# Attention scores from split keys: the second products on half the array's rows, copies of keys in place of copies of queries, and a new order

## The chip, the cores and the metric

The kernel runs on one core of one Trainium2 chip. The metric is device time in microseconds (us) of one execution. A core has TensorE (PE in the profile; PEld are its weight loads), VectorE (DVE), ScalarE (ACT), GpSimd (POOL), and SyncE (SP), whose queue issues nearly all of this kernel's transfers.

## The reference

The program is a sliding-window attention with sinks, followed by a two-layer network. All of it is float32.

```python
batch, n_heads, seq, head_dim = (4, 8, 768, 64)
n_sink, window = (4, 128)
scores = scale * np.matmul(q, k.transpose(0, 1, 3, 2))
keep = is_sink | in_window                  # first 4 keys, or the last 128 keys up to this one
scores = np.where(keep, scores, -1000000000.0)
a = softmax over keys;  x = a @ v           # heads side by side: 3072 tokens x 512
h = x @ w_in                                # 512 x 1024
solu = h * softmax(h);  ln = layer norm of solu, times g_ln
out = ln @ w_out                            # 1024 x 512
```

## The kernel before

**Tiles.** The work is cut into 24 windows `n` of 128 tokens: four batches of six. A window looks at its own 128 keys, the 128 keys before and the four sinks. So a score row of one head has 264 columns: two segments of `SEG` = 132 (four sink columns and 128 keys each). The first window of a batch has 128 columns alone.

**Split float32.** Each float32 factor is written as two numbers of the type fp32r, a first part (rounded to that type) and a second part (what is left), and a product is a sum of products of parts. A head has 64 dimensions, and the array has 128 rows, so two parts of a head fit above each other.

- `take_q` (ScalarE) writes the first part of four heads' queries into 64 rows of the tile `qT`, `rest_q` (VectorE) their second part into the other 64 rows. `x` (0 or 1) says which half holds the first part; `row_of` maps a head to `x` and its place `r`.
- `take_k` (ScalarE) and `rest_k` (GpSimd) do the same for keys in `ring`, a tile with four slots for windows' keys.
- `swap_q` copies `qT` with its halves exchanged into `qX`, by two DMAs of SP.
- `score` multiplies twice for each head, each time with 128 rows: `qT` by `ring` (first by first plus second by second), then `qX` by `ring` (second by first plus first by second). Both add into one bank of PSUM.

The first windows of batches 0 and 1 (`native`) are scored in plain float32 with 64 rows instead, by `qf` and `kf` (L654).

**After the scores.** There are two banks for scores, `bank_0` and `bank_1`; `claim` takes one and `done` gives it back. `pick` (L663) and `mask` (L674), both VectorE, merge the two segments, add the mask and find the row's maximum; then the bank is free. `exps` (ScalarE), `normalise` (GpSimd), a transposition of the probabilities (by DMA and VectorE, `store_p`, `load_p`, `flip_p`, or by TensorE), and `value` (L795), which multiplies by the values with 64 columns of the array for each of two heads. `hidden` (L815) and `project` (L902) are the network's two layers, three products of 512 columns for each block of weights.

**Order.** Every step is a function of `(n, i)`. A table of numbers, `ORDER`, lists all steps, and each engine runs its instructions in that order. So products of `hidden` and `project` of earlier windows stand between the scores of later ones.

Of the kernel before, what the change touches and what calls it, by code (L numbers as in the profile page):

```python
# [216 lines left out]
def _banded(ctx, tc, q, k, v, n_sink, window, w_in, w_out, g_ln, out, val, wts, wpool, consts):  # L217
# [264 lines left out]
    for b in range(B):  # L482
        upper = 1 if b == 1 else 0
        for c in range(NC):
# [6 lines left out]
            else:  # L491
                free = [x for x in (2 * up, 2 * up + 1) if (2, 0) not in slots or b > 1 or x != slots[2, 0]]
                slots[b, c] = free[c // 2 % len(free)]

    ring = cpool.tile([P, H, 4, SEG], F32R, name="ring")
    nc.vector.memset(ring.bitcast(F32)[:, :, 2:4, 0:NSK], 0.0)

    def slot_of(n):
# [622 lines left out]
```

## Time and profile before

| | |
|---|---|
| Time, median of 3 runs | 439.52 us (438.94 to 439.88) |
| The profiled execution | 439.91 us, of which the span is 437.9 us |
| TensorE busy | 415.4 us (95%) |
| VectorE busy | 360.9 us (82%) |
| ScalarE busy | 315.7 us (72%) |
| GpSimd busy | 234.2 us (53%) |
| DMA queue q1 | 80.77 MB, 82.3% of 16 engines' span |

The profile is of one execution. Busy times count an instruction from its start to its modelled end; products of TensorE overlap, so their rate is read from the distances of their starts. A row of the timeline gives the start in us from the span's start, the duration, the engine, the line and operation, `out<-in`, the part of the array (rows\*columns), shape, and how many instructions it merges; in brackets stands the idle time ahead of it and what ended it. A product of plain float32 leaves two records.

### The profile page before, as it was taken

To read this page: it belongs to the slowest core of one execution; us is meant where nothing else is said; L and a number is where in the kernel's file an instruction comes from. 1 tells how busy PE (TensorE), PEld (TensorE's weight loads), DVE (VectorE), ACT (ScalarE), POOL (GpSimd) and SP (SyncE) were. 2 spreads that over 40 slices of the span, in tenths; PEclk is the share of its full clock that TensorE was granted. 3 is DMA by queue.
4 is the path that set the end of the run, shared out by engine and by line. 5 is a ranking of instruction groups with operands and counts; after the bars stand their busy time and mean duration, and the time that the engine had idled before them with its cause. 6 is when DMAs were issued, how large, how long until landed. Compare 5 with 4: busy or idle time off the path is not lost.

```text
span 437.9 us, 8516 instructions
## 1 busy us (share of the span) xinstructions
PE 415.4 (95%) x2507; PEld 332.6 (76%) x2507; DVE 360.9 (82%) x1029; ACT 315.7 (72%) x817; POOL 234.2 (53%) x388
## 2 busy tenths in 40 slices
PE   4899999999999999999999999999999999999994
PEld 3447777878787888878777787878878778888884
DVE  2989999997999889999989997899899797674520
ACT  5989988978877776877768576768767675555551
POOL 7742626658867552788454736556623673624020
PEclk9999999999999999999999999999999999999999
DMA  8999449999899899976998989966966558623001
GB/s 225 324 284 293 96 101 168 180 151 196 218 161 216 208 185 253 195 229 190 180 239 210 207 219 226 193 173 179 269 176 216 170 165 227 188 96 121 24 26 55
DMA packets 164025, 81.38 MB, mean 186 GB/s; under 512 B 120188, under 2 KB 150788, under 8 KB 163972
## 3 DMA queue, kind: packets, MB, share of 16 engines
q1 hardware_dynamic: 163972, 80.77, 82.3%
q8 instruction: 22, 0.36, 0.4%
q14 instruction: 31, 0.25, 0.2%
HBM read 45.62 MB, written 23.72 MB: 158 GB/s over the span
## 4 chain that ended last, share of the span: by engine, by line
PE 53%; DVE 25%; DMA 6%; issue 5%; POOL 4%; ACT 4%; SPq 1%; DVEq 0%; POOLq 0%; ACTq 0%
PE o L902 18%; PE h L815 17%; PE av L795 5%; DVE qT L600 4%; DVE sc L674 3%; DVE bank L663 3%; PE bank L656 3%; PE bank L657 2%; PE ws L443 2%; DMA pb<-pd 2%; DVE ul L890 2%; DVE nm L820 2%; PE bank L654 2%; DMA wraw<-in_moe_w_in_dram 1%; DVE pt L725 1%
## 5 line engine op out<-in xcount | busy, mean ns | idle before, releaser
L685 ACT ACTIVATE sc<-sc,nmx 128x132 f32<-128x132 f32 (+1 forms) x192 | 75.9, 396 | 25.1 <-DVE nmx L674 24.1
L902 PE MATMUL o<-w2h,uh 128*128 128x512 f32 (+1 forms) x200 | 79.7, 398 | 0.0
L815 PE MATMUL h<-w1h,xh 128*128 128x512 f32 x192 | 77.0, 401 | 1.0 <-DVE u L830 0.9
L902 PE MATMUL o<-w2h,ul 128*128 128x512 f32 (+1 forms) x200 | 77.0, 385 | 0.5 <-DVE ul L890 0.5
L902 PE MATMUL o<-w2l,uh 128*128 128x512 f32 (+1 forms) x200 | 77.2, 386 | 0.0
L815 PE MATMUL h<-w1h,xl 128*128 128x512 f32 x192 | 75.9, 395 | 0.6 <-DVE xl L804 0.5
L815 PE MATMUL h<-w1l,xh 128*128 128x512 f32 x192 | 75.3, 392 | 0.0
L625 POOL TENSOR_TENSOR ring<-kf,ring 64x512 fp32r<-64x512 f32 x48 | 63.1, 1320 | 22.6 <-ACT ring L620 18.7
L674 DVE CUSTOM_DVE_ANT_0 sc<-bank,bias 128x132 f32<-128x132 f32 (+1 forms) x192 | 53.1, 288 | 9.4 <-PE bank L654 1.7
L704 POOL TENSOR_TENSOR pn<-sc,rs 128x512 f32<-128x512 f32 x26 | 28.0, 1079 | 53.1 <-DVE rs L691 19.2
L656 PE MATMUL bank<-ring,qT 128*128 128x264 f32 (+1 forms) x176 | 51.0, 300 | 1.9 <-DVE nmx L674 1.7
L657 PE MATMUL bank<-ring,qX 128*128 128x264 f32 (+1 forms) x176 | 48.3, 284 | 0.1
L700 POOL TENSOR_TENSOR sc<-sc,rs 128x528 f32<-128x528 f32 (+1 forms) x22 | 24.8, 1127 | 40.8 <-DVE rs L691 24.0
L902 PEld LDWEIGHTS o<-w2h,ul 128*128 128x128 f32 x200 | 37.5, 188 | 9.2 <-DVE ul L890 1.2
L902 PEld LDWEIGHTS o<-w2h,uh 128*128 128x128 f32 x200 | 37.6, 188 | 8.8 <-issue 3.1
L741 POOL TENSOR_SCALAR_AFFINE_SELECT pc<-pt 128x512 f32<-128x512 f32 x40 | 28.4, 716 | 29.4 <-DVE pt L725 25.5
L815 PEld LDWEIGHTS h<-w1h,xl 128*128 128x128 f32 x192 | 36.0, 188 | 10.6 <-DVE xl L804 2.8
L656 PEld LDWEIGHTS bank<-ring,qT 128*128 128x128 f32 x176 | 33.1, 188 | 12.0 <-DVE nmx L674 6.3
L815 PEld LDWEIGHTS h<-w1h,xh 128*128 128x128 f32 x192 | 36.1, 188 | 7.3 <-issue 0.8
L902 PEld LDWEIGHTS o<-w2l,uh 128*128 128x128 f32 x200 | 37.7, 188 | 5.0
L825 ACT ACTIVATE e<-h,nm 128x1024 f32<-128x1024 f32 x24 | 26.7, 1113 | 18.7 <-DVE nm L820 18.6
L815 PEld LDWEIGHTS h<-w1l,xh 128*128 128x128 f32 x192 | 36.2, 188 | 5.0
(146 smaller groups left out, 975.9 us busy)
## 6 DMA issues: line engine op xcount, KB each, us to landing
qX<-qT SPq DMA_DIRECT2D x88, 128.0 KB, 2.7
ud<-u SPq DMA_DIRECT2D x20, 512.0 KB, 4.3
ub<-ud SPq DMA_DIRECT2D x80, 128.0 KB, 3.5
pd<-pn SPq DMA_DIRECT2D x26, 256.0 KB, 3.0
pb<-pd SPq DMA_DIRECT2D x52, 128.0 KB, 3.4
vn<-in_v_dram SPq DMA_DIRECT2D x24, 256.0 KB, 4.3
out_dram<-ob SPq DMA_DIRECT2D x23, 256.0 KB, 2.6
kn<-in_k_dram SPq DMA_DIRECT2D x12, 384.0 KB, 6.6
```

The costliest lines, as they stand in the source:

```text
L625: nc.gpsimd.tensor_tensor(t[ROWS[1 - x]], src[ROWS[x]], t[ROWS[x]].bitcast(F32), op=ALU.subtract)
L656: nc.tensor.matmul(o, st["qT", n, x][:, r, :], rhs, start=True, stop=False)
L657: nc.tensor.matmul(o, st["qX", n, x][:, r, :], rhs, start=False, stop=True)
L674: nc.vector.tensor_tensor_reduce(out=st["sc", n, hb][:, j, c0:c1], in0=st["s", n, h].rearrange("p a x -> p (a x)")[:, c0:c1], in1=bias0 if ...
L685: nc.scalar.activation(sc[:, i, c0:c1], sc[:, i, c0:c1], AF.Exp, bias=nmx[:, i:i + 1], scale=-1.0, accum_out=ssum[:, i:i + 1])
L700: nc.gpsimd.tensor_tensor(sc[:, :, c0:c1], sc[:, :, c0:c1], rs.unsqueeze(2).to_broadcast([P, HB, c1 - c0]), op=ALU.mult)
L704: nc.gpsimd.tensor_tensor(pn.rearrange("p g h f -> p h g f"), sc[:, :, 4:SEG].rearrange("p h (g f) -> p h g f", f=32), rs.unsqueeze(2).uns ...
L741: nc.gpsimd.affine_select(pc, st["pt", n, hb], pattern=[[0, HB], [1, P]], compare_op=ALU.is_ge, fill=0.0, base=0, channel_multiplier=-1)
L795: nc.tensor.matmul(acc[ROWS[x], r, :], vals[:, 2 * r + x, :], p[:, 2 * jp + x, :], start=alone, stop=alone or (r, i) == (NPAIR - 1, 1))
L815: nc.tensor.matmul(st["h", n][:, cols], a[:, kt, :], w[:, kt, cols], start=(kt == 0 and m == 0), stop=(kt == KT1 - 1 and m == 2))
L825: nc.scalar.activation(e, st["h", n], AF.Exp, bias=st["nm", n], scale=1.0, accum_out=se)
L902: nc.tensor.matmul(st["o", n, i], a[:, kt % 4, :], part(w, kt)[:, i * wide:(i + 1) * wide], start=(kt == 0 and m == 0), stop=(kt == KT2 - ...
```

## The change

**Keys.** `ring` now holds the first part of a key in both halves: `take_k` writes one half, and the new `swap_k` copies it into the other by one DMA. The second part goes to a new tile, `ring_lo`, with each of two heads in its own half of the rows. `qX` and `swap_q` are gone.

**Scores.** `score` multiplies once with 128 rows: `qT` by `ring` (first by first plus second by first). The new step `cross` runs for a pair of heads, one in each half of the rows: two products of 64 rows, the first part of the queries by `ring_lo` (first by second). Second by second is left out of the sum.

**Heads.** For a pair, the two heads must stand in different halves; `row_of` now alternates in every window, `spot` finds a head's place afterwards, and `value` and `sinks_hi`/`sinks_lo` read their tiles by it. `skt` has one buffer instead of two. `ring_sinks` also copies the sink columns of `ring_lo`.

**Order.** `ORDER` is another table. On TensorE, before, in the middle of the kernel, a head's two products stand together, with products of `hidden` (`h`) around them:

```order
L815 MATMUL h_2219<-w1h,xl_2215 128x512
L656 MATMUL bank_89<-ring,qT_0_2017 128x264
L657 MATMUL bank_89<-ring,qX_0_2032 128x264
L815 MATMUL h_2219<-w1h,xh_2190 128x512
L815 MATMUL h_2219<-w1l,xh_2190 128x512
L815 MATMUL h_2219<-w1h,xl_2215 128x512
```

One bank is filled at a time. After, two heads' first products fill both banks, and the two products of 64 rows (L679, by `ring_lo`) follow:

```order
L674 MATMUL bank_89<-ring,qT_1_2019 128x264
L674 MATMUL bank_90<-ring,qT_0_2169 128x264
L679 MATMUL bank_90<-ring_lo,qT_0_2169 128x264
L679 MATMUL bank_89<-ring_lo,qT_1_2019 128x264
L842 MATMUL h_2261<-w1h,xh_2242 128x512
L842 MATMUL h_2261<-w1l,xh_2242 128x512
L842 MATMUL h_2261<-w1h,xl_2254 128x512
```

The second products of a pair moved together, behind both first ones. On SP, before, in the middle of the kernel, pairs of query copies stand between the other transfers:

```order
L867 DMA ub_2097<-ud_2022 32x4x256
L609 DMA qX_0_2228<-qT_0_2165 64x512
L610 DMA qX_0_2228<-qT_0_2165 64x512
L609 DMA qX_1_2237<-qT_1_2170 64x512
L610 DMA qX_1_2237<-qT_1_2170 64x512
L913 DMA out_dram<-ob_0_2172 128x512
```

After, single copies within `ring` stand there:

```order
L736 DMA pd_2151<-pn_0_2119 512x1x128
L631 DMA ring<-ring 64x4x128
L940 DMA out_dram<-ob_0_2159 128x512
L894 DMA ub_2198<-ud_2140 32x4x256 x2
```

Four copies for a window became two, on the keys' side.

The diff, without the rest of the table and the steps that only follow the heads' new places:

```diff
 ORDER = (
-    346, 0, 143, 2, 144, 244, 60, 348, 351, 5, 6, 3, 69, 350, 7, 51, 8, 352, 24, 9, 147, 154, 345, 12, 42, 155, 353,
...
+    ring_lo = cpool.tile([P, NPAIR, 4, SEG], F32R, name="ring_lo")
...
     def row_of(n, h):
-        return divmod(h, 2)[::-1] if turned(n) else divmod(h, NPAIR)
+        return divmod(h, 2)[::-1]
...
+    def spot(n, h):
+        return h if place(n)[0] == 0 else h % NPAIR * 2 + h // NPAIR
...
-    def swap_q(n, x):
-        if native(n):
-            return
-        t = st["qT", n, x]
-        o = st["qX", n, x] = sb.tile([P, NPAIR, P], F32R, tag="qX", name=f"qX_{n}_{x}", bufs=3)
-        nc.sync.dma_start(o.bitcast(F32)[0:D], t.bitcast(F32)[D:P])
-        nc.sync.dma_start(o.bitcast(F32)[D:P], t.bitcast(F32)[0:D])
...
+    def swap_k(n, x):
+        t = keys_of(n, x).bitcast(F32)
+        nc.sync.dma_start(t[ROWS[1 - x]], t[ROWS[x]])
+
     def rest_k(n, x):
-        t = keys_of(n, x)
         src = st["kf" if turned(n) else "kt", n]
-        nc.gpsimd.tensor_tensor(t[ROWS[1 - x]], src[ROWS[x]], t[ROWS[x]].bitcast(F32), op=ALU.subtract)
+        nc.gpsimd.tensor_tensor(ring_lo[ROWS[x], :, slot_of(n), 4:SEG], src[ROWS[x]],
+                                keys_of(n, x)[ROWS[x]].bitcast(F32), op=ALU.subtract)
...
+            nc.gpsimd.tensor_copy(ks[:, H:], ring_lo[:, :, first, 4:4 + NSK].bitcast(F32))
...
+                    nc.gpsimd.tensor_copy(ring_lo[:, :, slot, 0:NSK], st["ksink", b][:, H:].bitcast(F32))
...
+    def operands(n, h):
+        slot = slot_of(n)
+        x, r = row_of(n, h)
+        s = st["s", n, h]
+        if place(n)[1] == 0:
+            return s[:, 0, 4:SEG], ring[:, h, slot, 4:SEG], ring_lo[ROWS[x], r, slot, 4:SEG]
+        pslot = slot_of(before(n))
+        s0, s1 = min(slot, pslot), max(slot, pslot)
+        both = slice(s0, s1 + 1, s1 - s0)
+        return s, ring[:, h, both, :], ring_lo[ROWS[x], r, both, :]
+
     def score(n, h):
...
         nc.tensor.matmul(o, st["qT", n, x][:, r, :], rhs, start=True, stop=False)
-        nc.tensor.matmul(o, st["qX", n, x][:, r, :], rhs, start=False, stop=True)
+
+    def cross(n, r):
+        for x in range(2):
+            o, _, rhs = operands(n, 2 * r + x)
+            nc.tensor.matmul(o, st["qT", n, x][ROWS[x], r, :], rhs, start=False, stop=True)
...
-            skt = st["skt", n] = sb.tile([P, NPAIR, P], F32R, tag="skt", name=f"skt_{n}", bufs=2)
+            skt = st["skt", n] = sb.tile([P, NPAIR, P], F32R, tag="skt", name=f"skt_{n}", bufs=1)
```

More of the change, by code (lines that the diff above doesn't have):

```diff
@@ L495, in _banded @@
     ring = cpool.tile([P, H, 4, SEG], F32R, name="ring")
+    ring_lo = cpool.tile([P, NPAIR, 4, SEG], F32R, name="ring_lo")
     nc.vector.memset(ring.bitcast(F32)[:, :, 2:4, 0:NSK], 0.0)
+    nc.vector.memset(ring_lo.bitcast(F32)[:, :, 2:4, 0:NSK], 0.0)
     def slot_of(n):
@@ L507, in row_of @@
     def row_of(n, h):
-        return divmod(h, 2)[::-1] if turned(n) else divmod(h, NPAIR)
+        return divmod(h, 2)[::-1]
     def heads_of(n, x):
-        return slice(x, H, 2) if turned(n) else slice(NPAIR * x, NPAIR * (x + 1))
+        return slice(x, H, 2)
+    def spot(n, h):
+        return h if place(n)[0] == 0 else h % NPAIR * 2 + h // NPAIR
     def load(n, i, nm, src):
@@ L519, in load @@
         if turned(n):
-            nc.sync.dma_start(t.rearrange("p (c h d) -> p c h d", h=H, d=D)[:, region(n)],
-                              src[b, :, c * P:(c + 1) * P, :].rearrange("h p d -> p h d"))
+            to = t.rearrange("p (c h d) -> p c h d", h=H, d=D)[:, region(n)]
+            rows = src[b, :, c * P:(c + 1) * P, :].rearrange("h p d -> p h d")
+            if b == 0:
+                nc.sync.dma_start(to, rows)
+                return
+            for x in range(2):
+                nc.sync.dma_start(to[:, heads_of(n, x)], rows[:, NPAIR * x:NPAIR * (x + 1)])
             return
@@ L524, in load @@
         nc.sync.dma_start(t.rearrange("p (m d) -> p m d", d=32)[32 * i:32 * (i + 1)],
-                          src[b, heads_of(n, x), :, 32 * y:32 * (y + 1)].rearrange("h (t p) d -> p (h t) d", p=32))
+                          src[b, NPAIR * x:NPAIR * (x + 1), :, 32 * y:32 * (y + 1)].rearrange("h (t p) d -> p (h t) d", p=32))
     def load_k(n, i):
@@ L631, in ring_sinks @@
             first = slots[b, 0]
-            ks = st["ksink", b] = sb.tile([P, H, NSK], F32R, tag="ksink", name=f"ksink_{b}", bufs=2)
-            nc.gpsimd.tensor_copy(ks, ring[:, :, first, 4:4 + NSK].bitcast(F32))
+            ks = st["ksink", b] = sb.tile([P, H + NPAIR, NSK], F32R, tag="ksink", name=f"ksink_{b}", bufs=2)
+            nc.gpsimd.tensor_copy(ks[:, 0:H], ring[:, :, first, 4:4 + NSK].bitcast(F32))
+            nc.gpsimd.tensor_copy(ks[:, H:], ring_lo[:, :, first, 4:4 + NSK].bitcast(F32))
             fresh = [first] + fresh
@@ L637, in ring_sinks @@
                 if slot < 2:
-                    nc.gpsimd.tensor_copy(ring[:, :, slot, 0:NSK], st["ksink", b].bitcast(F32))
+                    nc.gpsimd.tensor_copy(ring[:, :, slot, 0:NSK], st["ksink", b][:, 0:H].bitcast(F32))
+                    nc.gpsimd.tensor_copy(ring_lo[:, :, slot, 0:NSK], st["ksink", b][:, H:].bitcast(F32))
     def cols_of(c):
         return (4, SEG) if c == 0 else (0, OFF)
-    def score(n, h):
-        slot = slot_of(n)
-        pslot = slot if place(n)[1] == 0 else slot_of(before(n))
-        s0, s1 = min(slot, pslot), max(slot, pslot)
-        s = st["s", n, h] = claim(("s", n, h), 1)[:, 0:2 * SEG].rearrange("p (a x) -> p a x", x=SEG)
-        if place(n)[1] == 0:
-            o, rhs = s[:, 0, 4:SEG], ring[:, h, slot, 4:SEG]
-        else:
-            o, rhs = s, ring[:, h, s0:s1 + 1:s1 - s0, :]
+    def operands(n, h):
[8 more added lines that the diff above has]
+        return s, ring[:, h, both, :], ring_lo[ROWS[x], r, both, :]
+    def score(n, h):
+        st["s", n, h] = claim(("s", n, h), 1)[:, 0:2 * SEG].rearrange("p (a x) -> p a x", x=SEG)
+        o, rhs, _ = operands(n, h)
         x, r = row_of(n, h)
@@ L656, in score @@
         nc.tensor.matmul(o, st["qT", n, x][:, r, :], rhs, start=True, stop=False)
-        nc.tensor.matmul(o, st["qX", n, x][:, r, :], rhs, start=False, stop=True)
+    def cross(n, r):
+        for x in range(2):
+            o, _, rhs = operands(n, 2 * r + x)
+            nc.tensor.matmul(o, st["qT", n, x][ROWS[x], r, :], rhs, start=False, stop=True)
     def pick(n, h):
@@ L748, in part_old, with sinks_of, sink_part @@
                                     fill=0.0, base=-1, channel_multiplier=1)
+    def sinks_of(n, hb, t):
+        sk = st["sk", n]
+        if place(n)[0] == 0:
+            return sk[:, hb * HB:(hb + 1) * HB, t]
+        return sk.rearrange("p (x g j) t a s -> p x g j t a s", x=2, g=NHB)[:, :, hb, :, t].rearrange("p x j a s -> p j x a s")
+    def sink_part(n, hb):
+        sv = st["sc", n, hb][:, :, 0:NSK].unsqueeze(2).to_broadcast([P, HB, 2, NSK])
+        return sv if place(n)[0] == 0 else sv.rearrange("p (j x) a s -> p j x a s", x=2)
     def sinks_hi(n, hb):
@@ L753, in sinks_hi @@
                 st["sk", n] = sb.tile([P, H, 2, 2, 4], F32R, tag="sk", name=f"sk_{n}", bufs=1)
-            hs = slice(hb * HB, (hb + 1) * HB)
-            sv = st["sc", n, hb][:, :, 0:NSK].unsqueeze(2).to_broadcast([P, HB, 2, NSK])
-            nc.scalar.copy(st["sk", n][:, hs, 0], sv)
+            nc.scalar.copy(sinks_of(n, hb, 0), sink_part(n, hb))
     def sinks_lo(n, hb):
         if place(n)[1] > 0:
-            hs = slice(hb * HB, (hb + 1) * HB)
-            sk = st["sk", n]
-            sv = st["sc", n, hb][:, :, 0:NSK].unsqueeze(2).to_broadcast([P, HB, 2, NSK])
-            nc.gpsimd.tensor_tensor(sk[:, hs, 1], sv, sk[:, hs, 0].bitcast(F32), op=ALU.subtract)
+            nc.gpsimd.tensor_tensor(sinks_of(n, hb, 1), sink_part(n, hb), sinks_of(n, hb, 0).bitcast(F32), op=ALU.subtract)
     def turn_sinks(n, _):
@@ L788, in value @@
         acc = accumulator(n)
-        for r in range(NPAIR):
-            hb, jp = divmod(r, HB // 2)
-            terms = [(n, st["pt" if alone else "pc", n, hb])] + ([] if alone else [(before(n), st["pt", n, hb])])
-            for i, (m, p) in enumerate(terms):
+        for r in sorted(range(NPAIR), key=lambda r: spot(n, 2 * r)):
+            for i in range(1 if alone else 2):
                 for x in range(2):
-                    vals = st["vo", n] if i and ("vo", n) in st else st["vn", m]
-                    nc.tensor.matmul(acc[ROWS[x], r, :], vals[:, 2 * r + x, :], p[:, 2 * jp + x, :],
+                    hb, j = divmod(spot(n, 2 * r + x), HB)
+                    p = st["pc" if i == 0 and not alone else "pt", n, hb]
+                    vals = st["vn", n] if i == 0 else st["vo", n] if ("vo", n) in st else st["vn", before(n)]
+                    nc.tensor.matmul(acc[ROWS[x], r, :], vals[:, 2 * r + x, :], p[:, j, :],
                                      start=alone, stop=alone or (r, i) == (NPAIR - 1, 1))
@@ L928, in _banded @@
     stages = {
-        load_k: loads, load_q: loads, load_v: 1, turn_q: 1, turn_k: 1, take_q: 2, rest_q: 2, swap_q: 2, keep_k: 1, take_k: 2,
-        rest_k: 2, ring_sinks: 1, score: H, pick: H, mask: H, exps: NPAIR, invert: NHB, normalise: NHB, turn_p: kept(NHB),
+        load_k: loads, load_q: loads, load_v: 1, turn_q: 1, turn_k: 1, take_q: 2, rest_q: 2, keep_k: 1, take_k: 2, swap_k: 2,
+        rest_k: 2, ring_sinks: 1, score: H, cross: lambda n: 0 if native(n) else NPAIR, pick: H, mask: H, exps: NPAIR, invert: NHB, normalise: NHB, turn_p: kept(NHB),
         take_p: kept(NHB), store_p: carries(NHB), load_p: carries(4), flip_p: carries(NHB), part_new: NHB, part_old: NHB, sinks_hi: NHB, sinks_lo: NHB, sink_values: 1, turn_sinks: 1,
```

268 rows, old and new, of the table ORDER are left out of this document.

## The prediction

> **What bounds the kernel now.** I read the page first: busy shares, granted clock, the chain that ended last, the costliest groups.
>
> ```profile
> span 437.9 us, 8516 instructions
> PE 415.4 (95%) x2507; PEld 332.6 (76%) x2507; DVE 360.9 (82%) x1029; ACT 315.7 (72%) x817; POOL 234.2 (53%) x388
> PEclk9999999999999999999999999999999999999999
> PE 53%; DVE 25%; DMA 6%; issue 5%; POOL 4%; ACT 4%; SPq 1%; DVEq 0%; POOLq 0%; ACTq 0%
> PE o L902 18%; PE h L815 17%; PE av L795 5%; DVE qT L600 4%; DVE sc L674 3%; DVE bank L663 3%; PE bank L656 3%; PE bank L657 2%; PE ws L443 2%; DMA pb<-pd 2%; DVE ul L890 2%; DVE nm L820 2%; PE bank L654 2%; DMA wraw<-in_moe_w_in_dram 1%; DVE pt L725 1%
> ...
> L674 DVE CUSTOM_DVE_ANT_0 sc<-bank,bias 128x132 f32<-128x132 f32 (+1 forms) x192 | 53.1, 288 | 9.4 <-PE bank L654 1.7
> ...
> L656 PE MATMUL bank<-ring,qT 128*128 128x264 f32 (+1 forms) x176 | 51.0, 300 | 1.9 <-DVE nmx L674 1.7
> L657 PE MATMUL bank<-ring,qX 128*128 128x264 f32 (+1 forms) x176 | 48.3, 284 | 0.1
> ```
>
> TensorE bounds the kernel: it is busy 95% of the span at the full granted clock, and 53% of the chain that ended last runs over it. VectorE is a close second with 25% of the chain. The two score products (L656, L657) are 176 each. Their 300 and 284 ns are latencies of a pipelined engine, so they don't give the rate. That is read from starts, in the timeline of TensorE (start, duration, then the group):
>
> ```profile
> 121.75 0.28 PE L656 MATMUL bank<-ring,qT 128*128 128x264 f32 x1
> 121.87 0.29 PE L657 MATMUL bank<-ring,qX 128*128 128x264 f32 x1
> 121.99 0.39 PE L815 MATMUL h<-w1h,xh 128*128 128x512 f32 x1
> 122.22 0.39 PE L815 MATMUL h<-w1l,xh 128*128 128x512 f32 x1
> ```
>
> A 264-column score product takes 0.12 us from start to start, a 512-column product 0.23 us. By stage:
>
> ```profile
> 120.00:160.00 40.00, 39.12 (x242) 32.35 (x240) 35.92 (x104) 29.31 (x81) 24.00 (x42) 1.00 1.13 197
> 200.00:240.00 40.00, 39.31 (x228) 31.48 (x228) 37.09 (x116) 30.04 (x82) 20.98 (x32) 1.00 1.04 209
> ```
>
> The columns are span, then busy time of TensorE, its weight loads, VectorE, ScalarE, GpSimd. In the middle of the kernel both TensorE (39 of 40 us) and VectorE (36 to 37) are close to full, so neither can take on work unnoticed.
>
> **The change, part by part.**
>
> *Second products: two of 128 rows become two of 64 rows.* Per pair of heads, two products of L657 go: 2 x 0.12 = 0.24 us. In their place stand two products of 64 rows on the two halves of the array. Whether such halves run beside each other is seen in the first scores of the kernel (L654), which have 64 rows and run by one head and by two:
>
> ```profile
> 28.36 0.49 PE L654 MATMUL bank<-kf,qf 64*128 64x128 f32 x2
> 28.77 0.66 PE L561 MATMUL bank<-ident,kn 128*128 128x128 f32 x4
> ```
>
> ```profile
> 32.69 0.49 PE L654 MATMUL bank<-kf,qf 64*128 64x128 f32 x4
> 33.11 0.66 PE L732 MATMUL ptp<-ident,sc 128*128 128x128 f32 x4
> ```
>
> One head leaves two records, two heads leave four, and both take 0.49 us, with the next product 0.41 and 0.42 us behind the first. So two heads cost 0.01 us more than one: they do run beside each other. A pair's second products therefore need 0.12 + 0.01 = 0.13 us of streaming, 0.11 less than before. If that were all, 88 pairs would save 88 x 0.11 = 9.7 us.
>
> *The array is split and joined around each pair.* This is what decides. The value products (L795) split the array too, by columns, once per chunk, and show the price at every edge:
>
> ```profile
> 111.47 0.40 PE L784 MATMUL av<-skt,vsink 128*128 128x512 f32 x1
> 111.80 0.44 PE L795 MATMUL av<-pc,vn 128*64 128x128 f32 x4
> 112.06 0.39 PE L795 MATMUL av<-pt,vn 128*64 128x128 f32 x4
> 112.28 0.39 PE L795 MATMUL av<-pc,vn 128*64 128x128 f32 x4
> ...
> 113.37 0.39 PE L795 MATMUL av<-pt,vn 128*64 128x128 f32 x4
> 113.69 0.50 PE L902 MATMUL o<-w2h,uh 128*128 128x512 f32 x1
> 114.03 0.39 PE L902 MATMUL o<-w2l,uh 128*128 128x512 f32 x1
> 114.26 0.40 PE L902 MATMUL o<-w2h,ul 128*128 128x512 f32 x1
> ```
>
> ```profile
> 113.69 0.19 PEld L902 LDWEIGHTS o<-w2h,uh 128*128 128x128 f32 x1 [0.17 <-issue]
> ```
>
> Entering: L784 has 512 columns, and 0.33 us pass before the next start instead of 0.23, so 0.10 lost. First split group: 0.26 instead of 0.22, 0.04 lost, the weight load that could not be done ahead. Leaving: 0.32 instead of 0.22, 0.10 lost. First whole product after it: 0.34 instead of 0.23, 0.11 lost, again its weight load. The load row shows the same thing: weights of L902, ready long before, are not loaded until the array is empty, and the idle time before them is put down to nothing that the profile shows. Sum 0.35 us for a split by columns with weights of 64 columns. The rows split of L654 fits: 0.41 us for one head is two slots of 0.11 (the av groups show 0.22 for two) plus 0.19, which is a full load of 128 columns (0.10) and the way out (0.10, rounded). With the way in at 0.10 and the next load at 0.11, one excursion costs about 0.10 + 0.10 + 0.10 + 0.11 = 0.41 us.
>
> The Trainium skill, "TensorEngine Tiling (Array Packing)", section "Key Properties", says that a change of tiling mode, not of tile alone, drains the engine; it gives no time for it. Its section "Theoretical Speedup" promises up to 2x for a contraction of 64 rows. By the second rule alone the sum would be the 9.7 us saved above; by the first, with this trace's price, it is the loss that follows. The trace agrees with both.
>
> So a pair's second products take 0.13 + 0.41 = 0.54 us instead of 0.24: 0.30 us more. The order of the changed kernel has 88 such pairs (80 of 264 columns and 8 of 128), each right behind its two first products. In five places the value products follow at once, which saves one return to the whole array, about 0.2 us each. TensorE gets 88 x 0.30 - 5 x 0.2 = 25.4 us more to do. The bounds: 9.7 us less if nothing is lost at the edges, 25.4 more.
>
> *First products.* 176 stay, with the same shape; the keys in both halves change what is summed, not the time. Zero.
>
> *How much of it lies on the path.* At least the share of the chain that is TensorE or issue, 53% + 5% = 58%: 14.7 us. At most all: 25.4. The nearest rows are those of the chain, and to TensorE's share I add VectorE's pick and mask, which start when a pair ends (L674 and L663, 3% of the chain each): 64%. The rest of the chain is VectorE work and transfers that the change leaves alone, and which gain slack. 0.64 x 25.4 = 16.3 us.
>
> *Both score banks held by a pair.* There are two banks; a pair keeps both until VectorE has read them, per head
>
> ```profile
> L663 DVE COPY_PREDICATED bank<-m_cur,bank 128x128 f32<-128x128 int32 x88 | 24.2, 285 | 7.7 <-PE bank L657 7.2
> L674 DVE DVE_READ_ACCUMULATOR2_ANT nmx<- 128x1 f32 x192 | 15.8, 82 | 0.0
> L820 DVE TENSOR_REDUCE nm<-h 128x1 f32<-128x1024 f32 x24 | 29.2, 1217 | 2.3 <-PE h L815 2.2
> ```
>
> 285 + 288 + 82 = 655 ns, so 1.31 us for two. The next pair's first products wait for the first bank. In all but four places the new order has at least six 512-column products in between, 6 x 0.23 = 1.38 us, which cover it if VectorE comes at once; the cover is thin where VectorE has a long step ahead, such as L820 with 1.2 us. Between 0 and 88 x 0.1 = 9 us; I take 0, since the longer pair itself leaves VectorE free meanwhile.
>
> *Copies.* 88 copies of queries go; 48 copies of keys come, plus two more loads for the one chunk of batch 1 that is prepared early. All issue on SP:
>
> ```profile
> qX<-qT SPq DMA_DIRECT2D x88, 128.0 KB, 2.7
> ```
>
> ```profile
> 313.68 3.40 DMA qX<-qT
> ```
>
> Each moves as much as one before, in shorter runs (four of 512 bytes in a partition instead of one of 2 KB). On the chain the query copies show at 313.68 with 3.40 us. A gain of up to 3.4 us, or a loss of as much if a key copy comes late in its place; the order issues them about a chunk ahead. I take 0. SP has 38 issues fewer, and nobody queues behind them.
>
> *GpSimd, ScalarE.* The remainder of the keys (L625) goes into its own tile with the same shape, and stays at its time; the sink columns get 12 more small copies:
>
> ```profile
> L625 POOL TENSOR_TENSOR ring<-kf,ring 64x512 fp32r<-64x512 f32 x48 | 63.1, 1320 | 22.6 <-ACT ring L620 18.7 <-POOL pt L747 1.0 <-POOL sk L763 0.6
> L638 POOL CAST ring<-ksink 128x32 fp32r<-128x32 f32 x8 | 1.5, 212 | 0.3
> L633 POOL CAST ksink<-ring 128x32 fp32r<-128x32 f32 x4 | 1.3, 328 | 0.1
> ```
>
> 12 x 0.21 to 0.33 = 2.5 to 4 us on an engine that is busy 53%: hidden. If they weren't, four of the batches' first windows would each start 0.6 to 1 us later.
>
> The profiled execution took 439.9 us, 0.4 above the median of 439.5. 439.9 + 16.3 = 456.2, which I round to 456.
>
> **The rivals.**
>
> *No loss at the edges (faster).* If rows of this type and 64-row halves switch without emptying the array, or the loads are pulled ahead, the 9.7 us stay saved; with 64 to 100% on the path, 6.2 to 9.7 us: 430 to 434. For it: the halves do overlap. Against it: both kinds of split in this trace lose 0.1 us on leaving, and the wait at 113.69 is on nothing but the array. It decides when one excursion costs under 0.11 us, against the 0.41 read here. The Trainium skill's page named above, by its speedup table alone, would side with this one. Chance 0.13.
>
> *The new order pays for most of it.* TensorE's waits in the old order vanish behind the longer pairs, and VectorE's share of the chain, 25%, sets the pace: 440 to 451. For it: VectorE at 36 to 37 of 40 us and transfers on the chain. Against: TensorE at 39 of 40, with little waiting to give up. Chance 0.20, of which 0.04 ends within 0.2% of the time before and 0.01 faster.
>
> *Banks held in pairs bind (slower still).* TensorE waits for VectorE after most pairs, 88 x 0.1 = 9 us on top of the full 25.4 x 0.64 to 25.4: 465 to 474. For it: cover of 1.38 against 1.31 us. Chance 0.07.
>
> **How the numbers follow.** The main case, 452 to 465, has 0.60; its point is 456. The range 440 to 465 leaves out the faster rival (0.13) and the one with banks (0.07), 0.2 together. About 0.2% (0.9 us) is what a measurement can tell here. Faster 0.14, within 0.2% 0.04, slower 0.82.
>
> **What would show it.** In the profile after: the pairs of 64-row products start within 0.01 us of each other; the product behind them starts about 0.3 us later and the one after that 0.34 later; weight loads behind the pairs show idle time put down to issue, 88 times about 0.2 us. TensorE's weight loads' idle time grows by some 25 us, and its share of the chain rises, VectorE's falls. I am wrong if the product behind a pair starts 0.13 us after it, or if the span grows by under 5 us with the edges as read.

## The result

The changed kernel takes 451.34 us (median of 4 runs, 451.25 to 451.81) against 439.64 us before (4 runs): a ratio of 1.0271, with an interval of 1.0253 to 1.0289. It is slower by 11.7 us. Run again later beside other kernels it gave 450.92 us and a ratio of 1.0249 (1.0215 to 1.0283).

The page of the profile after, in the lines that answer to those of before:

```profile
span 450.1 us, 8368 instructions
PE 432.7 (96%) x2507; PEld 331.8 (74%) x2507; DVE 361.2 (80%) x1030; ACT 319.7 (71%) x817; POOL 237.2 (53%) x400
PE 74%; DVE 7%; ACT 6%; DMA 5%; POOL 4%; issue 2%; SPq 1%; POOLq 0%; DVEq 0%
PE o L929 28%; PE h L842 23%; PE av L822 8%; PE bank L679 5%; PE bank L674 4%; PE ptp L754 2%; DMA ring<-ring 2%; PE av L811 1%; POOL ring_lo L635 1%; DMA qn<-in_q_dram 1%; DMA wraw<-in_moe_w_out_dram 1%; PE bank L672 1%; DVE qT L615 1%; DVE sc L696 1%; DVE w2l L469 1%
```

VectorE does as much as before (361.2 us, 360.9 before), and so do ScalarE and GpSimd within 4 us. TensorE's busy time alone has grown, by 17.3 us, with the same number of products. Its share of the chain that ended last rose from 53% to 74%, and VectorE's fell from 25% to 7%: three quarters of the chain are now TensorE's own work.

The edges of the split, in TensorE's timeline after the change (start, duration, what; x2 merges two products):

```profile
227.74 0.39 PE L842 MATMUL h<-w1h,xl 128*128 128x512 f32 x1
227.97 0.41 PE L674 MATMUL bank<-ring,qT 128*128 128x264 f32 x2
228.31 0.39 PE L679 MATMUL bank<-ring_lo,qT 64*128 64x264 f32 x2
228.62 0.50 PE L929 MATMUL o<-w2h,uh 128*128 128x512 f32 x1
228.96 0.40 PE L929 MATMUL o<-w2l,uh 128*128 128x512 f32 x1
229.20 0.40 PE L929 MATMUL o<-w2h,ul 128*128 128x512 f32 x1
```

Two first products take 0.24 us from start to start, but 0.34 us pass before the pair of 64 rows starts: 0.10 for the way in. The pair needs 0.31 us, of which 0.12 is streaming: 0.19 for its weight load and the way out. The next product needs 0.34 instead of 0.23: 0.11 for its own load. That is 0.40 us for an excursion.

### The profile page after: what moved, and what is told of

Its sections match the earlier page's. It is cut to its first block, busy times and chain, and to the rows that moved or that the text cites. A ratio compares the mean times of both kernels' runs of the same rounds, so it can differ in the third digit from the quotient of the medians.

```text
span 450.1 us, 8368 instructions
## 1 busy us (share of the span) xinstructions
PE 432.7 (96%) x2507; PEld 331.8 (74%) x2507; DVE 361.2 (80%) x1030; ACT 319.7 (71%) x817; POOL 237.2 (53%) x400
## 4 chain that ended last, share of the span: by engine, by line
PE 74%; DVE 7%; ACT 6%; DMA 5%; POOL 4%; issue 2%; SPq 1%; POOLq 0%; DVEq 0%
PE o L929 28%; PE h L842 23%; PE av L822 8%; PE bank L679 5%; PE bank L674 4%; PE ptp L754 2%; DMA ring<-ring 2%; PE av L811 1%; POOL ring_lo L635 1%; DMA qn<-in_q_dram 1%; DMA wraw<-in_moe_w_out_dram 1%; PE bank L672 1%; DVE qT L615 1%; DVE sc L696 1%; DVE w2l L469 1%
## 5 line engine op out<-in xcount | busy, mean ns | idle before, releaser
L929 PE MATMUL o<-w2h,uh 128*128 128x512 f32 (+1 forms) x200 | 83.1, 415 | 0.0
L842 PE MATMUL h<-w1h,xh 128*128 128x512 f32 x192 | 80.4, 419 | 0.4 <-ACT w2h L458 0.4
L929 PE MATMUL o<-w2l,uh 128*128 128x512 f32 (+1 forms) x200 | 77.3, 387 | 0.4 <-DVE w2l L469 0.4
L929 PE MATMUL o<-w2h,ul 128*128 128x512 f32 (+1 forms) x200 | 76.9, 384 | 0.0
L842 PE MATMUL h<-w1h,xl 128*128 128x512 f32 x192 | 76.2, 397 | 0.0
L842 PE MATMUL h<-w1l,xh 128*128 128x512 f32 x192 | 75.7, 394 | 0.0
L635 POOL TENSOR_TENSOR ring_lo<-kf,ring 64x512 fp32r<-64x512 f32 x48 | 64.7, 1350 | 8.3 <-ACT ring L627 5.7
L726 POOL TENSOR_TENSOR pn<-sc,rs 128x512 f32<-128x512 f32 x26 | 29.1, 1117 | 48.7 <-DVE rs L713 32.9
L929 PEld LDWEIGHTS o<-w2h,uh 128*128 128x128 f32 x200 | 37.5, 187 | 12.8 <-issue 3.1
L842 PEld LDWEIGHTS h<-w1h,xh 128*128 128x128 f32 x192 | 36.0, 188 | 11.5 <-ACT w2h L458 0.6
L929 PEld LDWEIGHTS o<-w2h,ul 128*128 128x128 f32 x200 | 37.5, 188 | 8.2 <-DVE ul L917 0.3
L674 PE MATMUL bank<-ring,qT 128*128 128x264 f32 (+1 forms) x176 | 41.0, 296 | 2.5 <-DVE nmx L696 1.1
L842 PEld LDWEIGHTS h<-w1h,xl 128*128 128x128 f32 x192 | 36.0, 188 | 9.2 <-DVE xl L831 0.9
L929 PEld LDWEIGHTS o<-w2l,uh 128*128 128x128 f32 x200 | 37.7, 188 | 5.8 <-DVE w2l L469 0.9
L674 PEld LDWEIGHTS bank<-ring,qT 128*128 128x128 f32 x176 | 32.1, 188 | 12.9 <-issue 2.1
L842 PEld LDWEIGHTS h<-w1l,xh 128*128 128x128 f32 x192 | 36.2, 188 | 6.2
L707 ACT ACTIVATION_READ_ACCUMULATOR sc<-sc,nmx 128x1 f32 x192 | 36.2, 188 | 0.0
```

The costliest lines, as they stand in the source:

```text
L635: nc.gpsimd.tensor_tensor(ring_lo[ROWS[x], :, slot_of(n), 4:SEG], src[ROWS[x]], keys_of(n, x)[ROWS[x]].bitcast(F32), op=ALU.subtract)
L674: nc.tensor.matmul(o, st["qT", n, x][:, r, :], rhs, start=True, stop=False)
L707: nc.scalar.activation(sc[:, i, c0:c1], sc[:, i, c0:c1], AF.Exp, bias=nmx[:, i:i + 1], scale=-1.0, accum_out=ssum[:, i:i + 1])
L726: nc.gpsimd.tensor_tensor(pn.rearrange("p g h f -> p h g f"), sc[:, :, 4:SEG].rearrange("p h (g f) -> p h g f", f=32), rs.unsqueeze(2).uns ...
L842: nc.tensor.matmul(st["h", n][:, cols], a[:, kt, :], w[:, kt, cols], start=(kt == 0 and m == 0), stop=(kt == KT1 - 1 and m == 2))
L929: nc.tensor.matmul(st["o", n, i], a[:, kt % 4, :], part(w, kt)[:, i * wide:(i + 1) * wide], start=(kt == 0 and m == 0), stop=(kt == KT2 - ...
```

## The experiments

The cuts show the main edit of each run; notes behind `#` and names such as `low` (the third result of `operands`) stand for lines that are left out.

**Whole rows in the new order.** The second products use all 128 rows of the same tiles. The sum gets one more term, the queries' second part by the second part of the other head's keys, which is small.

```diff
-            nc.tensor.matmul(o, st["qT", n, x][ROWS[x], r, :], rhs, start=False, stop=True)
+            nc.tensor.matmul(o, st["qT", n, x][:, r, :], rhs, start=False, stop=True)   # rhs: ring_lo[:, r, ...]
```

> The changed kernel with its order, its keys and its pairs, but the second products take all 128 rows of the same tiles, so that the array is never split for them. (Each sum then holds one more term, second part of the queries by the second part of the other head's keys.) Theory A, the edges of the split cost TensorE 31 us, streaming two heads side by side saves 10.7, and the waits that TensorE had in the old order paid 8 of it: the time falls by 20.6 and the 8 us of waits come back, 439 us (437 to 442), the time before the change. Theory B, the whole price stood on the path and the new order and the fewer copies gave 8 to 13 us back: 430 us (428 to 432). Theory C, the banks held in pairs are what costs: no change, 450 us.

The 31 us and the 8 us in this text are counts over all products of the two traces: each distance between starts was parted into what the shape takes without a split (0.23 us for 512 columns, 0.12 for 264), up to 0.10 us for each edge or unhidden load, and the rest, which is waiting. By that count the change adds 31 us of edges and takes away 10 of streaming, and waiting falls from 35 to 27.5 us. The terms are estimates, known to about 2 us: parted by each shape's own usual distance instead, the same starts give 33 us of edges, 12 of streaming, and waits that fall by 9, from 44 to 35.

Measured: 439.39 us (438.50 to 440.93), a ratio of 0.9975 (0.9948 to 1.0001) to before. Theory A holds, and theory C falls, since pairs hold both banks here as they do in the changed kernel. With the array whole, the rest of the change (pairs, key copies, new order) is worth nothing that can be told from zero, and the split costs all of the 11.7 us. Its timeline and chain:

```profile
227.56 0.41 PE L674 MATMUL bank<-ring,qT 128*128 128x264 f32 x2
227.80 0.41 PE L679 MATMUL bank<-ring_lo,qT 128*128 128x264 f32 x2
228.04 0.39 PE L842 MATMUL h<-w1h,xh 128*128 128x512 f32 x1
```

```profile
PE 41%; DVE 18%; DMA 14%; ACT 10%; POOL 7%; issue 5%; SPq 4%; DVEq 0%; POOLq 0%; ACTq 0%
```

Four products in 0.48 us, where the changed kernel needs 0.65 and 0.11 more behind it: 0.28 us for each pair.

**Twice as many excursions.** Each head's 64-row product comes right behind its first product, in `score` instead of in `cross`.

```diff
         nc.tensor.matmul(o, st["qT", n, x][:, r, :], rhs, start=True, stop=False)
+        nc.tensor.matmul(o, st["qT", n, x][ROWS[x], r, :], low, start=False, stop=True)
```

> The changed kernel, but each head's second product of 64 rows comes right behind its first product: 176 excursions into the split array instead of 88, and no two products beside each other. Theory A and B: 88 x (0.38 for the edges + 0.11 for the product that no longer runs beside another) = 43 us more for TensorE, nearly all of it on the path, because it has hardly a wait left: 490 us (482 to 496). Theory C: a bank is free earlier, so 445 us or less.

Measured: 488.69 us (488.47 to 488.95), 37.4 us above the changed kernel. Theories A and B had 490, theory C 445 or less. The trace gives TensorE 43 us more to do than in the changed kernel, as expected, and 6 us less waiting.

```profile
231.67 0.28 PE L674 MATMUL bank<-ring,qT 128*128 128x264 f32 x1
231.89 0.39 PE L675 MATMUL bank<-ring_lo,qT 64*128 64x264 f32 x1
232.21 0.39 PE L674 MATMUL bank<-ring,qT 128*128 128x264 f32 x1
232.52 0.39 PE L675 MATMUL bank<-ring_lo,qT 64*128 64x264 f32 x1
```

```profile
PE 91%; DVE 2%; ACT 2%; POOL 1%; DMA 1%; issue 1%; SPq 0%; DVEq 0%; POOLq 0%; ACTq 0%
```

Every change between whole and split array costs; the chain is TensorE's to 91%.

**The split in the old order.** The kernel before, its second products cut to 64 rows (first by second is left out).

```diff
-        nc.tensor.matmul(o, st["qX", n, x][:, r, :], rhs, start=False, stop=True)
+        nc.tensor.matmul(o, st["qX", n, x][ROWS[x], r, :], rhs[ROWS[x]], start=False, stop=True)
```

> The kernel before the change, order and copies as they were, but each head's second product takes only the 64 rows of the queries' second part by the keys' first part (first by second is left out). Columns and count are the same; the array is split 176 times. Theory A and B: 176 x 0.38 = 67 us more for TensorE, of which the 13 to 20 us of waits in the middle can pay some: 492 us (484 to 505). If only the number of rows counted: no change, 439 us.

Measured: 487.81 us (487.01 to 488.50), a ratio of 1.1072 (1.1022 to 1.1122). Half the rows, the same columns, no other edit: 47 us slower, or 0.27 us for each of 176 excursions. The loss needs neither the new order nor the pairs. Halves apart in the new order, above, are 49.3 us over whole rows in that order: with 176 excursions the price is the same in both orders within 2 us.

```profile
231.40 0.28 PE L656 MATMUL bank<-ring,qT 128*128 128x264 f32 x1
231.61 0.39 PE L657 MATMUL bank<-ring,qX 64*128 64x264 f32 x1
231.93 0.39 PE L656 MATMUL bank<-ring,qT 128*128 128x264 f32 x1
232.24 0.39 PE L657 MATMUL bank<-ring,qX 64*128 64x264 f32 x1
```

```profile
PE 93%; POOL 2%; DMA 1%; DVE 1%; ACT 1%; issue 1%; SPq 0%; POOLq 0%; ACTq 0%; DVEq 0%
```

Each step from a whole product to a 64-row one or back takes 0.21 to 0.32 us here, where two whole products stand 0.12 apart.

**Edges or products.** The pair's two products are issued twice in one excursion.

```diff
-        for x in range(2):
+        for x, last in ((0, False), (1, False), (0, True), (1, True)):
```

> The changed kernel with the two 64-row products of a pair issued twice in a row (the scores get the first part of the queries by the second part of the keys two times). If the price is paid at the edges, once for an excursion: 88 x 0.12 = 10.6 us more streaming, nearly all on the path, 461 us (458 to 463). If every product of 64 rows pays (an unhidden weight load or a slower product each): 88 x 0.3 to 0.4 = 26 to 35 us more, 477 to 486 us.

Measured: 463.01 us (461.17 to 463.64), 11.7 us above the changed kernel, for 88 pairs of products: 0.13 us each. The price is paid at the edges, once for an excursion.

```profile
219.59 0.41 PE L674 MATMUL bank<-ring,qT 128*128 128x264 f32 x2
219.93 0.51 PE L679 MATMUL bank<-ring_lo,qT 64*128 64x264 f32 x4
220.37 0.50 PE L811 MATMUL av<-skt,vsink 128*128 128x512 f32 x1
```

```profile
PE 81%; DVE 8%; ACT 4%; issue 2%; POOL 2%; DMA 2%; SPq 1%; DVEq 0%; POOLq 0%; ACTq 0%
```

Four products take 0.44 us to the next start, two took 0.31: inside the split two heads do run beside each other, and a further pair costs only its streaming.

**No second products.** They are left out of the changed kernel.

> The changed kernel without its second products (the scores lose the first part of the queries by the second part of the keys). TensorE has 88 x 0.5 = 44 us less to do than after the change and 21 less than before it. Theory A: VectorE and the transfers bind instead, 425 us (420 to 431). Theory B: 451 - 44 = 407 us (403 to 412). Theory C: 450 us, since pairs hold their banks as before.

Measured: 437.08 us (434.46 to 440.26), a ratio of 0.9923 (0.9895 to 0.9952). TensorE has 88 x 0.24 = 21 us less to do than with whole rows, and the time falls by 2.3 us. All three expectations miss it, A by 12 us: below 439 us VectorE and the transfers hold the kernel, as its chain shows (of the longest of the ten executions, 440.26 us):

```profile
DVE 32%; PE 24%; DMA 17%; ACT 10%; issue 6%; POOL 5%; SPq 5%; DVEq 0%; POOLq 0%; ACTq 0%
```

**Half of the excursions.** Whole rows in even windows, 64 rows in odd ones (`if n % 2`).

> The kernel with whole rows (439.4 us) where every other window has its second products on 64 rows again: half of the excursions, so half of TensorE's 20.6 us. If waits absorb the first part and then stop doing so: less than half of the 11.9 us between that kernel and the changed one, 442 to 445 us. If every excursion costs the same share of its length: 445.4 us.

Measured: 444.78 us (444.61 to 445.89), 5.4 us above whole rows, and 6.6 below the changed kernel. The first half may cost slightly less than the second, but the difference is within the noise, and the two expectations lie too close together for this run to choose.

```profile
PE 62%; DVE 12%; ACT 9%; DMA 7%; POOL 5%; issue 3%; SPq 1%; DVEq 0%; POOLq 0%; ACTq 0%
```

**Banks.** With whole rows, each head's second product right behind its first; `ring_lo` is cleared once at the start.

```diff
+        nc.tensor.matmul(o, st["qT", n, x][:, r, :], low, start=False, stop=True)   # in score; cross is empty
```

> The kernel with whole rows, but each head's second product comes right behind its first, so a bank is full 0.24 us earlier and no pair holds both banks until both are done (the tile of second parts is cleared once at the start). Holding banks in pairs costs nothing: 439 us (437 to 441). It costs 0.1 us for each pair: 431 to 435 us.

Measured: 442.87 us (439.76 to 443.74), 3.5 us slower than pairs. Holding both banks costs nothing that this run can find. Why the other way is slower was not parted. The clearing at the start can't be all of it: the profiled executions differ by 4.8 us, and TensorE's products of `hidden` and `project` fall behind by 2 us within the first 100 us, and by another 3 only between 260 and 330.

**Copies.** Four kernels ask what the 40 copies fewer were worth. All start from the kernel with whole rows, but for the one in the old order. First, each key copy issued twice to the same place:

```diff
         nc.sync.dma_start(t[ROWS[1 - x]], t[ROWS[x]])
+        nc.sync.dma_start(t[ROWS[1 - x]], t[ROWS[x]])
```

> The kernel with whole rows, with every copy of keys issued twice (96 copies, about as many as the 88 of queries before). If the number of copies does not matter: 439 us (438 to 441). If the 40 copies fewer are a gain that something else of the change eats: 442 to 445 us.

Measured: 550.22 us (547.42 to 552.47). Both expectations miss it, because this was another experiment than meant. In this program SP waits on a semaphore until the first copy has landed before it issues the second to the same place, and everything behind it on SP waits along:

```profile
SPq L632 <- DMA ring<-ring: 138.5, 48, 6.3
```

48 waits, 138.5 us, 2.9 each: about one transfer's landing (2.5 us in the median here). The 111 us are not all waiting of SP: the granted clock was 0.91 in this run, where whole rows had 1.00, and TensorE was busy 448.6 us instead of 416.4 with the same products. So the copy was repeated into a place of its own:

```diff
+        spare = dr.tile([D, NPAIR, P], F32, tag="spare", name=f"spare_{n}_{x}", bufs=8)
+        nc.sync.dma_start(spare, t[ROWS[x]])
```

> The kernel with whole rows, with a second copy of the same keys behind every key copy, but into a place of its own in DRAM, so that no copy waits for another one's landing: 96 copies instead of 48. If the number of copies does not matter: 439 us (438 to 442). If SP's issue time and the bytes matter: 48 x 0.5 = 24 us of SP time, part of it on the chain, 445 us or more. If the 110 us of the copies issued twice to one place came from the bytes and not from the wait: 500 us or more.

> The changed kernel unaltered, on the chip of the other run here, to have it beside whole rows: 451 us (450 to 453) whatever the theory.

Measured: 451.28 us (449.78 to 453.17), 11.9 us over whole rows for 48 copies, 0.25 us each. The number of copies does matter, and the bytes do not explain the 111 us. The changed kernel beside it gave 450.92, as expected. The same in the kernel before, with 44 copies of half a query tile:

> The kernel before the change with 44 more copies, one of half a query tile into DRAM behind each pair of query copies. If an added copy costs 0.25 us in any order: 440 + 11 = 451 us (448 to 454). If the old order had room in its queue: 441 us (439 to 444).

Measured: 444.87 us (443.84 to 450.02), about 4 us, 0.1 us each. An added copy costs time in both kernels, less in the old one, where it is a copy of queries in place of keys. Last, no key copies at all: ScalarE writes the second half too.

```diff
         nc.scalar.copy(keys_of(n, x)[ROWS[x]], src[ROWS[x]])
+        nc.scalar.copy(keys_of(n, x)[ROWS[1 - x]], src[ROWS[x]])   # swap_k is empty
```

> The kernel with whole rows, with no key copies by DMA at all: ScalarE writes the keys' first part into both halves, by a second instruction of 64x512 behind the first (48 x 0.61 = 29 us more on ScalarE, which is busy 73%). If a key copy costs what an added one did (11.9 us for 48): 428 us (427 to 433), faster than both kernels. If only copies that the order does not reckon with cost time: 439 us (437 to 443).

Measured: 451.00 us (448.89 to 452.06). Both expectations miss it: without any split this kernel is as slow as the changed one.

```profile
PE 418.2 (94%) x2507; PEld 333.6 (75%) x2507; DVE 358.8 (80%) x1030; ACT 348.4 (78%) x865; POOL 236.2 (53%) x400
PE 52%; ACT 24%; DVE 12%; issue 4%; DMA 3%; POOL 3%; SPq 1%; DVEq 0%; ACTq 0%; POOLq 0%
```

29.5 us more on an engine that was busy 73% cost 11.6 us, net of what the 48 copies left out may have given back. ScalarE is 24% of the chain now, 10% with the copies.

## Why the prediction was right, and by how much it was off

**Direction and cause.** The direction and the mechanism of the main case came: slower, by the edges of the split. The run with whole rows shows it, since it takes away the split alone and gives back the time of before. The edge price was read at 0.41 us for an excursion from L654 and L795 and is 0.40 after. The size did not come as the main case had it: 451.34 lies 0.7 us under its 452 to 465 and 0.3 over the 440 to 451 of the rival that lets waits pay. The stated range of 440 to 465 holds it because it covers both.

The Trainium skill, "TensorEngine Tiling (Array Packing)", section "Key Properties", says that a change of tiling mode drains the engine. The old order with 64 rows agrees: 47 us for 176 excursions. The speedup that the same page gives in its section "Theoretical Speedup" is there too, inside the split (0.01 us between one head and two before, 0.13 us for a further pair after), and is smaller than the edges.

**The sum.** Forecast 25.4 us x 0.64 = 16.3, measured 11.7. Both terms were too large, and the floor of 14.7 us, the chain's 58% of 25.4, did not hold.

- *TensorE's added work.* I took every excursion as a clean one. (Not every pair stands right behind both of its first products, as the prediction has it: 60 of 88 do. The way in costs the same 0.10 us behind other products of 512 columns.) Counted over all starts it is 31 us of edges less 10 of streaming, 21 us, 0.35 us an excursion on average. Where the next product is a transposition its load costs 0.06 us instead of 0.11, but that is so behind five pairs only; the rest of the difference between 0.35 and 0.40 may lie in the count, which caps every edge at 0.10.
- *The share on the path.* 11.9 of 21 us is 0.57, where I had added VectorE's 6% to the chain's 58%. The chain's own 58% was the better figure. But no single share holds. By counts of TensorE's work like the one above the share rises with the load:

| step | TensorE's work, us | time, us | share | TensorE's part of the chain after the step |
|---|---|---|---|---|
| no second products to whole rows | +21 | +2.3 | 0.11 | 41% |
| whole rows to half of the excursions | +11 | +5.4 | 0.5 | 62% |
| from there to the changed kernel | +10 | +6.6 | 0.65 | 74% |
| its pairs issued twice | +11 | +11.7 | 1 | 81% |
| or its halves apart | +43 | +37.4 | 0.87 | 91% |

The second and third rows do not differ clear of the noise: the time of each step is known to 1 or 2 us. The first row, the two after it and the last two do differ from one another. The share of the chain at the old point told roughly what the next 20 us would cost, and nothing about gains: below the old point TensorE's time is worth a tenth.

**The rivals.** No loss at the edges: refuted by the three runs with more or fewer excursions. It would also have gained less than I wrote: 9.7 us of TensorE's time saved, at the share of 0.11, is about 1 us and not 6 to 10. Banks held in pairs: refuted. The loads of the first products waited 6.3 us in all for VectorE to free a bank before, and 1.3 after:

```profile
L656 PEld LDWEIGHTS bank<-ring,qT 128*128 128x128 f32 x176 | 33.1, 188 | 12.0 <-DVE nmx L674 6.3 <-issue 0.9 <-POOL ring L625 0.3
L674 PEld LDWEIGHTS bank<-ring,qT 128*128 128x128 f32 x176 | 32.1, 188 | 12.9 <-issue 2.1 <-DVE nmx L696 1.3 <-DVE wbits L440 1.3
```

The new order pays for most of it: this rival was partly right. Waits paid about 8 of the 21 us, but because TensorE was longer, not by the new order, for with whole rows in the new order the same count finds 35 us of waiting again. Nor does VectorE set the pace, with 7% of the chain.

**What I would have looked for.** The pair's starts and the 0.31 and 0.34 us behind it came as said. The idle time of the weight loads did not: I forecast some 25 us more, put down to issue. It is span less busy time, 105.3 us before and 118.3 after, so 13 more. The idle time ahead of the second products' loads rose from 4.3 us (L657) to 13.5, of which the profile puts 3.6 down to issue. Of the 88 products behind a pair, 63 are of L929 and L842 by the first part of the weights. Ahead of the loads of these two groups it rose by 8 us (the last two rows against the first two), and issue did not grow:

```profile
L902 PEld LDWEIGHTS o<-w2h,uh 128*128 128x128 f32 x200 | 37.6, 188 | 8.8 <-issue 3.1 <-ACT ob L908 0.2
L815 PEld LDWEIGHTS h<-w1h,xh 128*128 128x128 f32 x192 | 36.1, 188 | 7.3 <-issue 0.8 <-ACT qT L592 0.8 <-ACT xh L800 0.5
L679 PEld LDWEIGHTS bank<-ring_lo,qT 64*128 64x128 f32 x176 | 16.5, 183 | 13.5 <-issue 3.6
L929 PEld LDWEIGHTS o<-w2h,uh 128*128 128x128 f32 x200 | 37.5, 187 | 12.8 <-issue 3.1 <-ACT e L852 0.3
L842 PEld LDWEIGHTS h<-w1h,xh 128*128 128x128 f32 x192 | 36.0, 188 | 11.5 <-ACT w2h L458 0.6 <-ACT xh L827 0.2
```

**Copies at zero.** Not shown. The sum of copies, pairs and order is zero within 0.5%, but an added copy costs 0.1 to 0.25 us, so the copies are not free, as the prediction had it ("nobody queues behind them"). Even the sign of their part is open, since the two kinds are not alike: a copy of queries landed after 2.7 us in the median, a copy of keys after 3.7. At 0.1 us for each of the 88 that went and 0.25 for each of the 48 that came, about 9 us gained stand against 12 lost. What would part copies, pairs and order is the new scheme in the old order; that was not run, so this stays open.

## What to carry to other kernels

A split of the array pays only if one excursion holds much work: here 0.40 us at the edges must be earned back at 0.11 us for each pair of heads, so four pairs or more would have to stand in one excursion, and two banks hold one. Before saving on an engine, ask what its time is worth at the margin on that side: leaving work out (the scores' second products) showed a tenth, adding work a half and then nearly all. In a kernel with a fixed order, an engine at 70 to 80% is no free cover: ScalarE's 29 us cost 11.6.

## What the runs showed of the hardware that I had not expected

- Two transfers into the same place, one behind the other on SP: this program waits 2.9 us for the first to land before it issues the second, and holds up all that follows. With 48 such pairs the kernel took 111 us longer, part of it at a lower granted clock (0.91). With the second copy in a place of its own there is no such wait.
- In a split by rows the weight loads of the two halves run beside each other too: two loads start 0.003 us apart in the median, and by their records both together take as long as one of the whole array, 0.19 us.

```profile
216.56 0.19 PEld L679 LDWEIGHTS bank<-ring_lo,qT 64*128 64x128 f32 x2
216.88 0.19 PEld L811 LDWEIGHTS av<-skt,vsink 128*128 128x128 f32 x1
```
